# Holding more of a two-round decode kernel's last heads on the chip: values in PSUM, a shorter ring, a second kept record tail

## The chip, the cores and the metric

The kernel runs on one core of a Trainium2 chip. The metric is the device time of one execution in microseconds (us), the median of the runs shown. PE is the matrix engine (PEld its weight loads), DVE the vector engine, ACT the scalar engine, SP the engine that issues the loads.

## The reference

One token for each of 4 sequences goes through attention and an MLP, and then through the same two layers, with the same weights and caches, once more. Cut to what is computed:

```python
def _A_ref(x, k_cache, v_cache, wq, wo):       # 32 heads of 128, the last W = 1024 cached positions
    q = (x @ wq) by heads
    scores = einsum("bhqd,bhkd->bhqk", q, k[-W:]) * (Dh ** -0.5)
    return (einsum("bhqk,bhkd->bhqd", softmax(scores), v[-W:])) by rows @ wo
def _B_ref(x, w1, w2):
    return maximum(x @ w1, 0) @ w2             # 640 -> 1728 -> 640
for _ in range(2):
    x = x + _A_ref(_layernorm(x), k_cache, v_cache, wq, wo)
    x = x + _B_ref(_layernorm(x), w1, w2)
```

All numbers are f32. One head's query weights, keys, values and output weights for all four sequences make one record: 128 partitions of 9472 columns (`REC`), 4.85 MB. There are 32 records, so a round reads 155 MB of them and 8.85 MB of MLP weights.

## The kernel before

**Storage.** SBUF holds five whole records (`slot0` to `slot4`), a `ring` of 6912 columns and `kept`, the last 2176 columns of one more record. In a record the columns run `WQ` (640), `K` (4096), `V` (4096), `WO` (640). Head h of round 0 lies in slot h mod 5.

**Order.** Round 0 takes heads 0 to 31. Heads 27 to 31 stay in the five slots, so round 1 takes them first, and then 0 to 26. Round 0 therefore loads 32 records and round 1 loads 27, of which head 26 lacks the 2176 columns from `KEPT` on, which `kept` has held since round 0.

**Per head** the loop in the body (L421 to L434) does: scores of the next head (PE, `sc_ps`, 16 matmuls in the trace's count), its softmax (DVE maximum, ACT exponential), the values of this head (PE, `o_ps`), `picks` (four DVE operations that collect the blocks of `o_ps`), the query of the head after next (PE, `misc`), a transposing matmul, the output projection into `acc`, and the softmax weights of the next head (DVE). So the K part of a record is read one loop step before its V part. `busy` adds matmuls whose result nobody reads; in round 1 they stand in the first three steps only (L429).

**Loads.** `items` is the list of all loads in the order in which they are issued, all on SP's queue. `pump` issues the first one as soon as its place is no longer `live`; `done` takes columns off the list when the code that reads them last has been written. A load into used columns waits on the chip for that last reader. SP works in order: a load that waits holds up all loads behind it.

**Between the rounds** the MLP weights go through the ring (`MLP_RING`, eleven loads). Behind them come the first records of round 1: parts of head 0 go to the ring (`IN_RING`), and the rest of head 0 and heads 1 to 5 go, piece by piece, to the places that heads 27 to 31 leave (`places`); the last piece, the end of head 5, takes the ring. Head 6 is the first whole record again, in slot 2 (`home`), where head 27 was. Until then slot 2 holds pieces of heads 0, 1 and 2.

**PSUM** has eight banks of 512 columns: `sc_ps0` and `sc_ps1` (two each), `t_ps`, `o_ps`, `acc`, `misc`.

Of the kernel before, what the change touches and what calls it, by code (L numbers as in the profile page):

```python
# [58 lines left out]
RING = 4 * FF  # L59
KEPT = WO - 3 * 512  # L60

MLP_RING = [("w1", 1, 0), ("w1", 1, FF), ("w1", 1, 2 * FF), ("w1", 1, 3 * FF), ("w1", 1, 0), ("w2", 10, 1728),
            ("w2", 11, 3328), ("w2", 11, 5088), ("w2", 10, 0), ("w2", 8, 1728), ("w2", 4, 3008)]

IN_RING = [(512, 1664, 3648), (1664, 3712, 4800), (3712, 5248, 0), (0, 128, 1536), (5248, 6272, 1728),
           (6272, 6784, 2752), (128, 512, 3264)]
IN_SLOT = 6784
# [4 lines left out]
LATE = 5  # L72
# [24 lines left out]
def decode_kernel(ctx: ExitStack, tc: tile.TileContext, xf, rec, w1, w2, out):  # L97
# [24 lines left out]
    slot = [sb.tile([P, REC], F32, name=f"slot{i}") for i in range(NS)]  # L122
    ring = sb.tile([P, RING], F32, name="ring")
    kept = sb.tile([P, REC - KEPT], F32, name="kept")

# [41 lines left out]
    at = {("rec", 1, LAST - 1): [(KEPT, REC, "kept", 0)]}  # L167
    live = []
    buffers = dict(enumerate(slot)) | {"ring": ring, "kept": kept}

    def load(key, src, lo, hi, buf, col):
        items.append((key, src, lo, hi, buf, col))
# [4 lines left out]
    def ending(r, hs, late):  # L177
        a, b, c = hs[-3:]
        end = WO if late else REC
        last = WO if late else KEPT  # L180
        for h, lo, hi in ((a, 0, V), (b, 0, V), (a, V, end), (c, 0, V), (b, V, end), (c, V, V + VH), (c, V + VH, last)):
            piece(r, h, lo, hi)
        if late:
            for h in hs[-1:] + hs[-LATE:-1]:
                piece(r, h, WO, REC)
# [5 lines left out]
    for h in hs[1:-3]:  # L191
        piece(0, h, 0, KEPT if h == LAST - 1 else WO if h >= H - LATE else REC)
        if h == LAST - 1:
            piece(0, h, KEPT, REC, "kept", 0)
    ending(0, hs, True)
    loaded = {"w1": 0, "w2": 0}
    for name, size, col in MLP_RING:
        n, loaded[name] = loaded[name], loaded[name] + size * {"w1": FF, "w2": FD}[name]
        load((name, 0), {"w1": w1, "w2": w2}[name], n, loaded[name], "ring", col)
# [6 lines left out]

    for lo, hi, col in IN_RING:
        piece(1, new[0], lo, hi, "ring", col)
# [3 lines left out]
    stream = [(new[0], IN_SLOT, REC)] + [(h, 0, REC) for h in new[1:6]]  # L212
    for buf, lo, hi in places:
        while stream:
            h, c, end = stream[0]
            cut = max(x for x in [*CUTS, end] if x <= min(end, c + hi - lo))
            if cut <= c:
                break
            piece(1, h, c, cut, buf, lo)
            lo += cut - c  # L220
            stream[:1] = [(h, cut, end)] if cut < end else []
    for h in new[6:-3]:
        piece(1, h, 0, REC)
    ending(1, hs, False)
    for ks in W1_SLOT:
        load(("w1", 1), w1, ks[0] * FF, (ks[-1] + 1) * FF, home(LAST + 1, 0), ks[0] * FF)
    n = 0
    for size in W2_SLOT:
        load(("w2", 1), w2, n * FD, (n + size) * FD, home(LAST + 2, 0), n * FD)
# [23 lines left out]
    def done(key, lo, hi):  # L253
# [3 lines left out]
        for x, y, buf, col in pieces(key):  # L257
            a, b = col + max(lo, x) - x, col + min(hi, y) - x
            if a < b:
                rest = []  # L260
                for bb, u, v in live:
                    if bb != buf or v <= a or b <= u:
                        rest.append((bb, u, v))
                    else:
                        rest += [(bb, p, q) for p, q in ((u, a), (b, v)) if p < q]
                live[:] = rest
        pump()

# [4 lines left out]
    def busy(n, to=sc_ps[1], groups=1, h=LAST):  # L273
# [5 lines left out]
    def center(fill):  # L279
# [3 lines left out]
        if fill:  # L283
            busy(256, groups=fill)
        pe.matmul(misc[:, :B], sums.to_broadcast([P, P]), pick, start=True, stop=True)
        if fill > 1:
            busy(128, groups=2)
# [6 lines left out]
    def deviation(rows, bias, scale):  # L294

        pe.matmul(o_ps[:, 8:8 + B], ones.to_broadcast([P, P]), squares, start=True, stop=True)
        dve.tensor_tensor(mrt, o_ps[:, 8:8 + B], rows, op=OP.mult)
# [13 lines left out]
    def scores(r, h, s, first=False):  # L311
        key = ("rec", r, h)
        for i in range(2):
# [4 lines left out]
            if first and i == 0:  # L318
                deviation(of_batch, eps_dh, float(DH))
                act.activation(unused, eps, AF.Exp)  # L320
# [50 lines left out]
    def mlp(r):  # L371
# [3 lines left out]
        for k in range(KB):  # L375
            for j in range(NB):
                pe.matmul(h_ps[32 * j:32 * j + B, :FQ], xblock(k), cols(("w1", r), k * FF + FQ * j, FQ),
                          start=(k == 0), stop=(k == KB - 1))
            done(("w1", r), k * FF, k * FF + FF)
# [12 lines left out]
        key = ("w2", r)  # L392
        sizes = W2_SLOT if r else [size for name, size, _ in MLP_RING if name == "w2"]
        first = 0
        for i, size in enumerate(sizes):
            for s in range(first, first + size):
                m, n = TILES[s]
                w = cols(key, s * FD, FD)
# [5 lines left out]
            done(key, first * FD, (first + size) * FD)  # L404
# [5 lines left out]
    for r in range(2):  # L410
# [4 lines left out]
        if r:  # L415
            busy(256, groups=2)
        scores(r, hs[0], 0, True)
        softmax(0, True)
        query(r, hs[1])
        weights(0)  # L420
# [20 lines left out]
        values(r, hs[-1], 1, (1, 0))  # L441
        output_T(late - 2, by_act=True)
        picks(1)
# [50 lines left out]
```

## Time and profile before

| | us |
|---|---|
| median of 3 runs | 715.53 (715.3 to 715.67) |
| span of the profiled execution (first to last instruction) | 713.9 |
| busy: PE / DVE / ACT | 518.8 / 357.4 / 93.3 |
| share of the 16 DMA engines that SP's queue took | 99.0% |

The runs are timed from outside and lie 1.6 us above the profiled execution's span; a difference found in the span is carried over to the runs as it is. The profile page gives, by 40 slices, how busy each engine was and which share of its full clock PE was granted. The chain of waits follows the work that ended last back to the start. The timeline has single instructions with their start and duration, and windows give an engine's busy time, PE's granted clock and the DMA rate for any stretch. Line 89 (or 86) is the line of a helper through which every instruction is recorded, so instructions are told apart by their tiles.

### The profile page before, as it was taken

The numbers are of one execution on the slowest core, as the hardware profiler recorded it, in microseconds if no ns is written. First come the engines' busy times: TensorE is split into PE (matmuls) and PEld (weight loads), VectorE is DVE, ScalarE is ACT, GpSimd is POOL, SyncE is SP. The second block draws the span as 40 slices with busy tenths as digits, with TensorE's granted clock in tenths as the row PEclk, the third lists the DMA queues.
The fourth block names the chain that finished last, engine by engine and source line by source line (L and its number), as shares of the span: only waits on it lengthen the run. The fifth ranks groups of instructions, "written<-read, shape, count | busy, mean of one in ns | idle before, by whom it ended". The sixth has DMA issues, their size and how long they took to land.

```text
span 713.9 us, 8959 instructions
## 1 busy us (share of the span) xinstructions
PE 518.8 (73%) x3716; PEld 210.9 (30%) x3716; DVE 357.4 (50%) x1007; ACT 93.3 (13%) x147; POOL 1.1 (0%) x9
## 2 busy tenths in 40 slices
PE   4466858666785766868889998477767767686868
PEld 2131323223232231323224343132222313232323
DVE  3335445544454545446642887535444454445752
ACT  1201010110110101011111222101010110101111
POOL 0000000000000000000000000000000000000000
PEclk9768686877678677577899999857886687668989
DMA  9999999999999999999999999999999999999996
GB/s 374 442 437 430 425 436 440 429 419 442 438 432 423 434 438 437 417 442 422 424 406 408 428 429 429 442 438 423 430 439 436 427 430 434 437 430 423 429 424 274
DMA packets 16633, 303.38 MB, mean 425 GB/s; under 512 B 1856, under 2 KB 2384, under 8 KB 6736
## 3 DMA queue, kind: packets, MB, share of 16 engines
q1 hardware_dynamic: 16560, 302.80, 99.0%
q8 instruction: 29, 0.48, 0.2%
q14 instruction: 12, 0.10, 0.0%
q10 hardware_dynamic: 32, 0.01, 0.0%
HBM read 302.72 MB, written 0.08 MB: 424 GB/s over the span
## 4 chain that ended last, share of the span: by engine, by line
DMA 79%; PE 17%; DVE 2%; issue 1%; SPq 0%; ACT 0%
DMA slot<-rec 76%; PE sc_ps L89 6%; PE misc L89 5%; PE o_ps L89 4%; DMA ring<-w 3%; PE acc L89 3%; DVE scratch L89 1%; DVE oTs L89 1%; DVE small L89 0%; SPq L89 0%; DVE t_ps L89 0%; SPq L86 0%; DVE xT L89 0%; ACT oTs L89 0%; DVE qT L89 0%
## 5 line engine op out<-in xcount | busy, mean ns | idle before, releaser
L89 PE MATMUL misc<-xT,slot 128*128 128x4 f32 x630 | 103.2, 291 | 154.5 <-DMA slot<-rec 154.3
L89 PE MATMUL sc_ps<-slot,qT 128*4 128x512 f32 x1008 | 196.7, 920 | 1.0 <-DVE qT L89 1.0
L89 PEld LDWEIGHTS misc<-xT,slot 128*128 128x128 f32 x630 | 97.7, 240 | 210.8 <-DMA slot<-rec 199.1
L89 ACT ACTIVATE sc_ps<-sc_ps,small 128x1024 f32<-128x1024 f32 (+1 forms) x68 | 76.6, 1127 | 555.3 <-DVE small L89 554.8
L89 PE MATMUL o_ps<-slot,scratch 128*16 128x512 f32 x964 | 135.1, 672 | 3.0 <-DVE scratch L89 3.0
L89 DVE TENSOR_REDUCE small<-sc_ps 128x1 f32<-128x1024 f32 x64 | 78.3, 1223 | 73.9 <-PE sc_ps L89 73.9
L89 DVE STREAM_TRANSPOSE t_ps<-sc_ps 128x512 f32<-128x512 f32 x128 | 93.2, 728 | 2.1
L89 DVE COPY qT<-misc 128x4 f32<-128x4 f32 x64 | 10.2, 160 | 166.1 <-PE misc L89 166.1
L89 PEld LDWEIGHTS o_ps<-slot,scratch 128*16 128x16 f32 x964 | 32.7, 117 | 128.4 <-issue 79.0
L89 DVE SCALAR_TENSOR_TENSOR scratch<-o_ps,of_block,scratch 128x128 f32<-128x128 f32 x186 | 65.2, 351 | 6.6
L89 PEld LDWEIGHTS sc_ps<-slot,qT 128*4 128x4 f32 x1008 | 33.5, 115 | 84.1 <-issue 73.1
L89 PE MATMUL acc<-slot,oTs 128*4 128x160 f32 x488 | 36.5, 387 | 14.3 <-DVE oTs L89 14.0
L89 DVE TENSOR_SCALAR scratch<-o_ps,of_block 128x128 f32<-128x128 f32 x62 | 21.7, 351 | 34.1 <-PE o_ps L89 34.1
L89 PE MATMUL o_ps<-pick,scratch 128*128 128x4 f32 x124 | 29.1, 305 | 4.8 <-DVE scratch L89 4.8
L89 DVE TENSOR_TENSOR scratch<-t_ps,mrt 128x64 f32<-128x64 f32 x128 | 28.8, 225 | 4.7
L89 PEld LDWEIGHTS o_ps<-pick,scratch 128*128 128x128 f32 x124 | 26.1, 260 | 8.8 <-DVE scratch L89 7.5
L89 PE MATMUL sc_ps<-slot,small 128*1 128x256 f32 (+2 forms) x56 | 17.7, 462 | 0.0
L89 DVE COPY oTs<-o_ps 128x4 f32<-128x4 f32 x60 | 9.7, 162 | 14.8 <-PE o_ps L89 13.9
L89 DVE TENSOR_SCALAR mrt<-of_batch,small 128x4 f32<-128x4 f32 x64 | 14.7, 230 | 2.2
L89 DVE STREAM_TRANSPOSE scratch<-small 128x32 f32<-128x32 f32 x64 | 12.9, 201 | 2.4 <-ACT sc_ps L89 2.4
L89 PEld LDWEIGHTS acc<-slot,oTs 128*4 128x4 f32 x488 | 6.9, 84 | 19.5 <-DVE oTs L89 19.1
L89 ACT ACTIVATION_READ_ACCUMULATOR sc_ps<-sc_ps,small 128x1 f32 x64 | 12.2, 191 | 0.0
(71 smaller groups left out, 113.6 us busy)
## 6 DMA issues: line engine op xcount, KB each, us to landing
slot<-rec SPq DMA_DIRECT2D x43, 4736.0 KB, 30.7
slot<-rec SPq DMA_DIRECT2D x12, 2368.0 KB, 29.6
slot<-rec SPq DMA_DIRECT2D x2, 4416.0 KB
slot<-rec SPq DMA_DIRECT2D x2, 2304.0 KB, 18.4
ring<-w SPq DMA_DIRECT2D x5, 864.0 KB, 10.7
slot<-rec SPq DMA_DIRECT2D x2, 2112.0 KB, 19.0
slot<-rec SPq DMA_DIRECT2D x2, 2048.0 KB, 41.4
slot<-rec SPq DMA_DIRECT2D x4, 1024.0 KB, 20.3
```

The source lines that it names most:

```text
L89: r = build(*args, **kwargs)
```

## The change

1. `kept2`, a second tail of 2176 columns, takes the end of head 23 in round 0. Round 1 then loads head 23 without these columns.
2. The ring shrinks from 6912 to 4832 columns.
3. After the last values of round 0, `park` copies 1536 columns of head 31's values from slot 1 to PSUM (ACT, 1024 columns to `sc_ps1`, 512 to `o_ps`). Their place in slot 1 (`spare`) takes MLP weights and parts of head 0. At the start of round 1 `unpark` copies the columns to slot 2, into the K part that head 27 has just been read from (ACT 512 columns, DVE twice 512, and DVE clears `o_ps`). Head 31 reads them there.
4. The MLP's two weight arrays become one, `wm`, loaded in twelve pieces through ring and spare place; the lists of places follow. The end of `places` changes: columns of slot 2 that `unpark` used, and the spare columns of slot 1, are filled last, after head 31, with parts of head 5.
5. Six output projections of round 0 are kept for its end instead of five (`LATE`), head 26's among them.
6. What `busy`, `center` and `deviation` write goes to `misc` and `t_ps`, since `sc_ps1` and `o_ps` are taken.

```diff
-RING = 4 * FF
+RING = 4832
+PARKED = 1536
-LATE = 5
+LATE = 6
...
+    kept, kept2 = (sb.tile([P, REC - KEPT], F32, name=n) for n in ("kept", "kept2"))
...
-    at = {("rec", 1, LAST - 1): [(KEPT, REC, "kept", 0)]}
+    at = {("rec", 1, LAST - 1): [(KEPT, REC, "kept", 0)], ("rec", 1, LAST - 4): [(KEPT, REC, "kept2", 0)]}
+    spare = home(H - 1, 0)
...
     places = [(old[i], lo, hi) for i, lo, hi in (
-        (0, 0, K), (0, K, K + VH), (0, K + VH, V), (1, 0, K + VH), (1, K + VH, V), (0, V, WO), (0, WO, REC), (2, 0, V),
-        (1, V, REC), (3, 0, V), (2, V, REC), (4, 0, V), (3, V, REC), (4, V, REC))] + [("ring", 0, RING)]
+        (0, 0, K), (0, K + 1024, K + VH), (0, K + VH + 512, V), (1, 0, K + VH), (1, K + VH, V), (0, V, WO), (0, WO, REC),
+        (2, 0, V), (1, V, REC), (3, 0, V), (2, V, REC), (4, 0, V), (3, V, REC), (4, V + PARKED, REC),
+        (0, K, K + 1024), (0, K + VH, K + VH + 512), (4, V, V + PARKED))] + [("ring", 0, RING)]
...
     for h in new[6:-3]:
-        piece(1, h, 0, REC)
+        piece(1, h, 0, KEPT if h == LAST - 4 else REC)
...
+    def park(i):
+        if i == 0:
+            act.copy(sc_ps[1], slot[spare][:, V:V + 1024])
+        else:
+            act.copy(o_ps, slot[spare][:, V + 1024:V + PARKED])
+            free(spare, V, V + PARKED)
+            pump()
+
+    def unpark(i):
+        b = home(LAST, 0)
+        a = [K, K + 512, K + VH][i]
+        if i == 0:
+            act.copy(slot[b][:, a:a + 512], sc_ps[1][:, :512])
+        else:
+            dve.tensor_copy(slot[b][:, a:a + 512], [sc_ps[1][:, 512:], o_ps][i - 1])
+        live.append((b, a, a + 512))
+        if i == 2:
+            dve.memset(o_ps, 0.0)
```

SP's list at the point where whole records begin again in round 1. Before, the piece into the ring is the last of head 5, and head 6 follows into slot 2:

```order
L89 DMA slot1_71<-rec 128x4736
L89 DMA slot0_70<-rec 128x4224
L89 DMA slot0_70<-rec 128x512
L89 DMA ring_75<-rec 128x4224
L89 DMA slot2_72<-rec 128x9472
L89 DMA slot3_73<-rec 128x9472
```

And now; the two pieces of 1024 and 512 columns into slot 2 are keys of head 5 (the second half of its positions):

```order
L96 DMA slot1_71<-rec 128x3200
L96 DMA slot2_72<-rec 128x1024
L96 DMA slot2_72<-rec 128x512
L96 DMA slot1_71<-rec 128x1536
L96 DMA ring_77<-rec 128x3200
L96 DMA slot2_72<-rec 128x9472
L96 DMA slot3_73<-rec 128x9472
```

The load of head 6 is now behind two pieces of head 5 in the same slot, so it has to wait until PE has done the scores of head 5; before, the last reader of what slot 2 held was head 1's output projection.

DVE at the first softmax of round 1, before:

```order
L89 TENSOR_REDUCE small_69<-mrt_68 128x1
L89 TENSOR_REDUCE small_69<-sc_ps0_77 128x1
L89 RECIPROCAL small_69<-small_69 128x1
L89 TENSOR_TENSOR small_69<-small_69 128x1
L89 COPY qT_64<-misc_82 128x4
L89 STREAM_TRANSPOSE scratch_62<-small_69 128x32
```

And now:

```order
L96 TENSOR_REDUCE small_69<-mrt_68 128x1
L96 COPY slot2_72<-sc_ps1_79 128x512
L96 TENSOR_REDUCE small_69<-sc_ps0_78 128x1
L96 RECIPROCAL small_69<-small_69 128x1
L96 TENSOR_TENSOR small_69<-small_69 128x1
L96 COPY qT_64<-misc_83 128x4
L96 COPY slot2_72<-o_ps_81 128x512
L96 MEMSET o_ps_81 128x512
L96 STREAM_TRANSPOSE scratch_62<-small_69 128x32
```

One copy now stands ahead of the maximum over the scores, and a copy and a clearing stand between the copy of the next query and the first operation of the softmax weights.

More of the change, by code (lines that the diff above doesn't have):

```diff
@@ L191, in decode_kernel @@
     for h in hs[1:-3]:
-        piece(0, h, 0, KEPT if h == LAST - 1 else WO if h >= H - LATE else REC)
+        piece(0, h, 0, KEPT if h in (LAST - 4, LAST - 1) else WO if h >= H - LATE else REC)
+        if h == LAST - 4:
+            piece(0, h, KEPT, REC, "kept2", 0)
         if h == LAST - 1:
-            piece(0, h, KEPT, REC, "kept", 0)
+            piece(0, h, KEPT, WO, "kept", 0)
     ending(0, hs, True)
[L196 to L199, printed above, removed]
+    for lo, hi, buf, col in MLP_RING:
+        load(("w", 0), wm, lo, hi, buf, col)
     hs = order[1]
```

96 lines of the change are left out of this document (59 added, 37 removed).

## The prediction

> **What bounds the kernel now.** I read the page first, for the loads against everything else, then windows for their rate, then the chain and the timeline where round 1 starts.
>
> ```profile
> span 713.9 us, 8959 instructions
> ...
> DMA  9999999999999999999999999999999999999996
> ...
> q1 hardware_dynamic: 16560, 302.80, 99.0%
> ```
>
> The loads never stop: 302.80 MB, 99% of the 16 DMA engines over the whole span. Two windows give their rate, in the last column (GB/s; before it the DMA share and PE's granted clock):
>
> ```profile
> 40.00:300.00 260.00, 183.70 (x1204) 74.31 (x1196) 125.45 (x346) 29.78 (x46) 0.00 (x0) 0.74 1.00 432
> 0.00:453.20 453.20, 333.38 (x2394) 135.19 (x2398) 233.23 (x660) 62.04 (x97) 1.12 (x9) 0.80 1.00 427
> 370.00:380.00 10.00, 8.83 (x76) 2.17 (x74) 1.03 (x3) 2.32 (x5) 0.00 (x0) 1.00 0.98 398
> ```
>
> With whole records the rate is 432 GB/s, so one record of 4.85 MB takes 11.2 us. The time is bytes divided by rate, plus every moment in which the queue is empty. Such a moment hardly exists before; the nearest to one is in the MLP between the rounds (0.98).
>
> One stretch works the other way round: heads 27 to 31 need no loads, so at the start of round 1 PE and DVE set the pace and the loads run ahead into the places that they leave. The chain shows where that ends:
>
> ```profile
> 437.81 0.76 PE acc L89 x8
> 438.56 0.02 issue
> 438.58 27.80 DMA slot<-rec
> 466.38 0.04 issue
> 466.42 2.30 PE misc L89 x10
> ```
>
> At 438.58 head 1's projection frees slot 2, SP issues head 6, the first whole record, and its data land 27.80 us later. Of these 27.80 us only 11.2 are its own transfer; the rest is the queue ahead of it. That lead is what the change touches.
>
> **The bytes saved.** `kept2` spares round 1 2176 columns x 512 B = 1.114 MB. At 432 GB/s that is **2.58 us**. All other bytes stay, the weights in `wm` too. Nothing else in the change shortens the loads.
>
> **The new wait.** Head 6 now goes to slot 2 behind keys of head 5, and is issued only when the scores of head 5 are done. When is that, and when is the queue empty?
>
> PE's rows (start, duration; `sc_ps` are scores, `o_ps` values):
>
> ```profile
> 431.92 1.90 PE L89 MATMUL sc_ps<-slot,qT 128*4 128x512 f32 x16
> 438.30 3.30 PE L89 MATMUL sc_ps<-slot,qT 128*4 128x512 f32 x16
> 445.87 1.90 PE L89 MATMUL sc_ps<-slot,qT 128*4 128x512 f32 x16
> 452.04 1.90 PE L89 MATMUL sc_ps<-slot,qT 128*4 128x512 f32 x16
> ```
>
> These are the scores of heads 2, 3, 4 and 5. The last end at 453.94; heads follow each other every 6.17 us (445.87 to 452.04), and the waits of PE from 400 to 455 name no load, so this is a pace of PE and DVE that the loads don't set.
>
> Up to the last piece of head 5 the list before holds 188,608 KB = 193.1 MB. The window 0 to 453.20 at 427 GB/s is 193.5 MB: averaged over the engines, the queue reaches head 6 at 453.2, give or take 0.5 from the rounding. The changed list has the same bytes up to there (`kept2` saves behind it). So **the queue is empty at about 453.2, and the load that should follow is issued at about 454**: a lead of 14.6 us becomes less than nothing. Heads 7 and 8 are behind head 6 on SP and wait with it, though slots 3 and 4 are free by then; once it is issued, three records follow at once, and the queue is full again. So the loss is paid once.
>
> What does a restart cost from issue? Rows for an empty queue are the start and the end of the program (chain of the start, then the page of issues, us to landing last):
>
> ```profile
> 0.81 0.38 SPq L86
> ...
> 2.18 35.08 DMA slot<-rec
> ```
>
> ```profile
> out<-scratch SPq DMA_DIRECT2D x1, 80.0 KB, 1.6
> ```
>
> The small store lands after 1.6 us, 0.2 of them its transfer at 432 GB/s: 1.4. The first four loads (two of 2368 and two of 4736 KB, 14.55 MB, 33.7 us at that rate) are issued from 0.81 and land at 37.26: 2.8. The second holds the lag of the slowest engine, which a running queue has as well. I take 2.0 us, between them, and keep 1.4 and 2.8.
>
> [...]
>
> **What moves PE's 453.94.** Four small edits lie ahead of it:
>
> ```profile
> 364.13 0.16 ACT L89 COPY oTs<-o_ps 128x4 f32<-128x4 f32 x1 [4.86 <-PE o_ps L89]
> 369.66 1.28 ACT L89 ACT_TABLE_LOAD   x1 [5.37 <-DVE small L89]
> 390.95 0.29 ACT L89 ACTIVATE small<-small 128x1 f32<-128x1 f32 x1 [13.36 <-DVE small L89]
> 393.12 1.18 ACT L89 ACTIVATE sc_ps<-sc_ps,small 128x1024 f32<-128x1024 f32 x1 [0.35 <-DVE qT L89]
> 390.70 0.16 DVE L89 TENSOR_REDUCE small<-mrt 128x1 f32<-128x4 f32 x1
> 391.53 1.22 DVE L89 TENSOR_REDUCE small<-sc_ps 128x1 f32<-128x1024 f32 x1 [0.67 <-PE sc_ps L89]
> 394.44 0.21 DVE L89 STREAM_TRANSPOSE scratch<-small 128x32 f32<-128x32 f32 x1 [1.35 <-ACT sc_ps L89]
> 396.04 0.73 DVE L89 STREAM_TRANSPOSE t_ps<-sc_ps 128x512 f32<-128x512 f32 x1
> ```
>
> - `park`: no row is an ACT copy of this size; the exponential over 128x1024 takes 1.18, so 1.2 and 0.65 for the two. They fall into ACT's idle 4.86 and 5.37 us around 364: nothing. Without that cover the first would delay `oTs`, at most 1.2. The spare place is free near 365, when three weight loads are still queued.
> - `unpark`: a DVE copy of 128x512 lies between 0.16 (four columns) and 0.73 (the transpose of 512); I take 0.7. The first fills the gap from 390.86 to 391.53 and overhangs by about 0.1. The second, with the clearing of `o_ps` (no row; up to another 0.7), lies in the 1.35 us in which DVE waits for the exponential: 0 to 0.1. ACT's copy, 0.65 from about 390.1, ends before 390.95. Together **0.2** (0 to 0.7).
> - The ring and the spare place hold 6368 columns for weights where the ring held 6912, 0.64 us of transfer less. In the MLP SP then issues later against a queue that already had 0.98; the last weights can land up to 1 us later, though the late projections and fillers are waiting for loads there anyway. I take **0.1** (0 to 1.0). Idle time of the queue itself in that stretch costs nothing more, because it is empty at 453 in any case.
> - The sixth late projection, the merged weights and the other targets of the fillers change no sum: the same matmuls in the same idle time.
>
> Sum, against the profiled execution: 453.94 + 0.3, issue 0.06 after it, restart 2.0: data flow again at 456.3 where they flowed on at 453.2. That is 3.1 lost and 2.58 saved, **+0.5 us**, if PE meets the same clock.
>
> **PE's clock.** It need not. The row at 438.30 took 3.30 us where its like take 1.90, 1.4 us more. Windows of 3.41 us (clock in the column before the DMA share):
>
> ```profile
> 389.93:393.34 3.41, 2.91 (x28) 1.71 (x28) 1.85 (x6) 2.01 (x4) 0.00 (x0) 1.00 1.04 404
> 393.34:396.75 3.41, 3.41 (x20) 0.67 (x16) 2.17 (x6) 1.07 (x2) 0.00 (x0) 0.50 1.02 416
> 417.23:420.65 3.42, 2.74 (x32) 1.78 (x35) 2.80 (x11) 1.11 (x2) 0.00 (x0) 1.00 1.03 436
> 420.65:424.06 3.41, 3.41 (x33) 1.39 (x25) 3.05 (x8) 0.85 (x1) 0.00 (x0) 1.00 1.02 432
> 434.30:437.71 3.41, 2.83 (x24) 1.61 (x16) 2.67 (x9) 1.29 (x2) 0.00 (x0) 1.00 1.00 430
> 437.71:441.13 3.42, 3.32 (x24) 0.87 (x28) 2.36 (x8) 0.00 (x0) 0.00 (x0) 0.50 0.97 409
> 451.37:454.78 3.41, 3.15 (x38) 1.05 (x41) 3.06 (x9) 0.00 (x0) 0.00 (x0) 1.00 1.10 472
> ```
>
> The clock halves for whole windows on a grid of 3.41 us (393.34 + 13 x 3.413 = 437.71), here behind windows that hold much of the pause between a head's values and the next scores, 2.55 us in which PE has only small matmuls (449.49 to 452.04 in the rows). The busy column counts those too, so it doesn't show it. Where do windows lie against that pause?
>
> ```profile
> 415.15 1.90 PE L89 MATMUL o_ps<-slot,scratch 128*16 128x512 f32 x16
> 433.63 1.90 PE L89 MATMUL o_ps<-slot,scratch 128*16 128x512 f32 x16
> 447.59 1.90 PE L89 MATMUL o_ps<-slot,scratch 128*16 128x512 f32 x16
> ```
>
> The window that started 1.2 us before the values' end (434.30 against 435.53) was followed by a slow one; one that started 0.2 after it (417.23 against 417.05) was not, nor one 1.5 before it (447.95 against 449.49). So about 1.3 of 3.41 us of positions are bad. Two windows are 6.83, a head 6.17: the grid moves 0.66 per head, meets a bad position at the latest after five heads, is thrown back about two heads by the 1.4 us lost, and meets one again about three heads later. Six heads without fillers precede the scores of head 5. From a chance position that makes mostly two slow windows; the profiled execution had one, plus the one at 393.3, which I price at 0.35 because the values behind it waited for DVE's weights in any case. Before, none of this reached the end, since the queue had 14.6 us of lead. Now it does. I take two and none at 393: +0.5 + 1.4 - 0.35 = **+1.6 us**, so 715.5 + 1.6 = **717.1**.
>
> **The rivals.** 0.2% of this kernel is 1.43 us, about what a measurement of it can tell from no change.
>
> - *One slow window, as in the profile.* +0.2 without the one at 393, +0.5 with it: 715.7 to 716.0. For it: the one execution that is shown. Against: the count above. [...]
> - *Three slow windows, or one across the scores of head 5 themselves.* +1.6 + 1.4: about 718.5. Possible from positions that are bad at the first head.
> - *Faster: the queue hardly empties.* No slow window at all and a restart of 1.4: PE's scores end at 453.94 - 1.4 - 0.35 + 0.3 = 452.5, data flow at 454.0, 0.8 lost and 2.58 saved: -1.8, 713.7. It decides at about 1.1 us lost for a measurable gain. Against it: the drift argument leaves hardly a position without a slow window.
> - *The saving comes but the ring costs.* Weights land 1 us late and PE's pace with them, over the forecast: 718.1. Or the tail of head 23 isn't spared: +2.6 more; the list of loads speaks against that.
>
> **How the numbers follow.** Forecast (two slow windows) 0.45, one 0.20, three 0.22, hardly empty 0.10, ring 0.03. The forecast lies so near the bound that I give 0.27 of its 0.45 to slower and 0.18 to no change. Faster 0.10, same 0.18 + 0.20 = 0.38, slower 0.27 + 0.22 + 0.03 = 0.52. Range: from the one-window case with the short restart and no delay, 715.7 - 0.8 = 714.9, to three windows with 0.5 of the ring's cost, 719.0. The faster case and a tail above stay out. Its cases lie in steps of 1.4 us, so runs of the changed kernel should differ more among themselves than the 0.37 us before.
>
> **What would show it.** The SP row of the first whole record into slot 2 stands 0.06 behind PE's scores of head 5, near 454 to 456, no longer behind a projection at 438.6. The DMA share falls for 2 to 5 us there, and PE then waits for a load until about 468 to 470. The queue moves 301.7 MB. ACT's and DVE's copies take 0.6 to 1.2 us and the maximum at 391.53 starts 0.1 to 0.2 later. I am wrong if the share doesn't fall at 454 (the queue was longer than I think), if it falls in the MLP by several us, or if runs agree within 0.4 us while the wait is there.

## The result and the profile after

| | before | after |
|---|---|---|
| median, us | 715.60 (715.30 to 715.76, 5 runs) | 719.26 (718.38 to 720.90, 5 runs) |
| ratio | | 1.0053, 95% interval 1.0040 to 1.0065 |
| profiled execution: span | 713.9 | 716.6 (its time 718.40) |

The change makes the kernel 3.7 us slower by the medians and 2.7 us by the spans of the profiled executions. The forecast was 717.1, its range ended at 719.0. One execution of the kernel before, 769.65 us at a granted clock of 0.55, is in none of the numbers here.

The page after, in the rows that answer those of before:

```profile
span 716.6 us, 8970 instructions
...
DMA  9999999999999999999999999899999999999997
...
q1 hardware_dynamic: 16560, 301.69, 98.7%
```

The queue moves 1.11 MB less, as it should, and its row of tenths has one dip, in slice 26 of 40 (448 to 466 us). Microsecond windows there (last column GB/s):

```profile
453.00:454.00 1.00, 1.00 (x10) 0.95 (x9) 0.93 (x3) 1.00 (x2) 0.00 (x0) 1.00 1.03 441
454.00:455.00 1.00, 0.42 (x3) 0.30 (x2) 0.56 (x5) 0.02 (x1) 0.00 (x0) 1.00 0.84 358
455.00:456.00 1.00, 0.89 (x16) 0.43 (x20) 0.93 (x5) 0.00 (x0) 0.00 (x0) 1.00 0.51 218
456.00:457.00 1.00, 1.00 (x12) 0.22 (x8) 0.93 (x3) 0.00 (x0) 0.00 (x0) 1.00 0.27 106
457.00:458.00 1.00, 1.00 (x16) 0.27 (x12) 0.96 (x3) 0.00 (x0) 0.00 (x0) 1.00 0.00 0
458.00:459.00 1.00, 1.00 (x12) 0.08 (x4) 0.84 (x2) 0.00 (x1) 0.00 (x0) 1.00 2.04 568
```

From 454 on the share of the 16 engines that are busy falls step by step (0.84, 0.51, 0.27), and from 457 to 458 no packet starts. (A packet counts in the window in which it starts, so a share can exceed 1.) The chain of waits names the cause; before, a projection at 437.81 stood here, and 27.80 us of load behind it:

```profile
455.57 1.79 PE sc_ps L96 x16
457.37 14.08 DMA slot<-rec
471.49 2.30 PE misc L96 x10
```

Head 5's scores end, SP issues head 6, and PE gets the record 14.08 us later; 11.2 of them are its own transfer. This is the predicted wait. But the issue stands at 457.37, where 455.3 was forecast. PE's rows show why:

```profile
391.07 1.03 PE L96 MATMUL sc_ps<-slot,qT 128*4 128x512 f32 x8
...
433.56 3.60 PE L96 MATMUL sc_ps<-slot,qT 128*4 128x512 f32 x16
...
447.80 3.31 PE L96 MATMUL sc_ps<-slot,qT 128*4 128x512 f32 x16
...
455.38 1.90 PE L96 MATMUL sc_ps<-slot,qT 128*4 128x512 f32 x16
```

Two scores at half clock, as forecast (3.60 and 3.31 us instead of 1.90; the granted clock is 0.50 from 433.56 to 436.97 and 0.51 from 447.20 to 450.60). But round 1's first scores start at 391.07; before, they did 2.0 us earlier:

```profile
389.12 1.03 PE L89 MATMUL sc_ps<-slot,qT 128*4 128x512 f32 x8
```

So the two late microseconds come from ahead of round 1, from the MLP. Windows of that stretch, before and then after:

```profile
362.00:400.00 38.00, 34.79 (x332) 12.81 (x326) 13.66 (x47) 7.19 (x13) 0.00 (x0) 0.96 1.01 410
376.00:388.00 12.00, 11.38 (x146) 4.45 (x138) 1.99 (x7) 1.08 (x3) 0.00 (x0) 1.00 1.02 410
```

```profile
362.00:400.00 38.00, 31.72 (x320) 11.76 (x315) 13.11 (x41) 7.13 (x14) 0.00 (x0) 1.00 1.00 385
376.00:388.00 12.00, 9.91 (x132) 4.05 (x133) 0.87 (x2) 1.08 (x3) 0.00 (x0) 1.00 0.99 369
```

25 GB/s less over 38 us are 0.95 MB, 2.2 us of transfer. The DMA share (the column ahead of the rate) hides it: 1.01 against 1.00. A share near 1 is no proof that the queue is full; the rate tells more. The chain of that stretch, before and after:

```profile
380.02 5.84 DMA ring<-w
385.86 0.04 issue
385.90 0.53 PE acc L89 x8
```

```profile
377.46 6.71 DMA ring<-wm
384.21 1.39 PE acc L96 x34
```

Before, the last load of the MLP stands there, and 0.5 us of PE behind it. Now it is the largest, 2560 columns (1280 KB, 3.0 us of transfer), issued at 377.46. PE waits for the whole of it, then does 34 matmuls, the rest of the group, three more groups and the unread matmuls between them. The next load into these columns is issued at 385.78, when PE has nearly finished the group; before, the columns came free in smaller parts.

**Lead.** For each load I counted how much of the queue lay ahead of it when it was issued: the bytes listed ahead of it, less the bytes that the trace's packets had moved by then (a packet under way counts by the part of its time that has passed), divided by 432 GB/s. Of the 18 loads issued between 365 and 392 us before, none had less than 2.0 us of lead; the least was 2.1. After the change 3 of 14 had 1.1 to 1.7. The rate dips right behind these loads. After the change, behind the issues at 377.46 (lead 1.1) and at 385.78 (1.3):

```profile
376.50:378.00 1.50, 1.46 (x8) 0.26 (x8) 0.08 (x1) 0.50 (x2) 0.00 (x0) 1.00 0.98 408
378.00:380.00 2.00, 1.61 (x26) 0.74 (x27) 0.78 (x2) 0.57 (x2) 0.00 (x0) 1.00 0.97 318
386.50:388.00 1.50, 1.50 (x28) 0.75 (x28) 0.00 (x0) 0.00 (x0) 0.00 (x0) 1.00 1.06 332
```

Before, at the same place, and behind the load with the least lead (368.87, 2.1):

```profile
378.00:380.00 2.00, 1.80 (x30) 0.66 (x24) 0.07 (x1) 0.00 (x0) 0.00 (x0) 1.00 0.99 401
369.50:371.00 1.50, 1.50 (x10) 0.17 (x2) 0.08 (x1) 1.33 (x2) 0.00 (x0) 1.00 0.88 323
```

By 390 the changed kernel's queue had lost 1.7 us more than the one before, and 1.1 of them in the three stretches behind its short-lead loads (368 to 371, 378 to 380, 386 to 388). Smaller dips (372 to 373, 382 to 384) stand behind loads with more lead, so the count isn't the whole account, and the bound of 2.0 us is chosen with the traces at hand. The experiments ask whether short lead is what costs.

### The profile page after: what moved, and what is told of

Read it like the earlier page. It is cut to its first block, busy times and chain, and to the rows that moved or that the text cites. A ratio compares the mean times of both kernels' runs of the same rounds, so it can differ in the third digit from the quotient of the medians.

```text
span 716.6 us, 8970 instructions
## 1 busy us (share of the span) xinstructions
PE 514.7 (72%) x3718; PEld 210.3 (29%) x3718; DVE 358.6 (50%) x1010; ACT 95.5 (13%) x150; POOL 1.1 (0%) x9
## 3 DMA queue, kind: packets, MB, share of 16 engines
q1 hardware_dynamic: 16560, 301.69, 98.7%
## 4 chain that ended last, share of the span: by engine, by line
DMA 78%; PE 18%; DVE 3%; issue 1%; another core or an unknown queue 1%; ACT 0%; SPq 0%
DMA slot<-rec 72%; PE sc_ps L96 5%; PE misc L96 5%; PE o_ps L96 5%; DMA ring<-wm 3%; DMA slot<-wm 3%; PE acc L96 3%; DVE scratch L96 2%; DVE oTs L96 1%; DVE small L96 0%; ACT sc_ps L96 0%; PE t_ps L96 0%; DVE t_ps L96 0%; DVE mrt L96 0%
## 5 line engine op out<-in xcount | busy, mean ns | idle before, releaser
L96 PE MATMUL misc<-xT,slot 128*128 128x4 f32 x640 | 104.7, 290 | 157.0 <-DMA slot<-rec 156.7
L96 PE MATMUL o_ps<-slot,scratch 128*16 128x512 f32 x958 | 133.2, 661 | 3.7 <-DVE scratch L96 3.2
L96 PE MATMUL acc<-slot,oTs 128*4 128x160 f32 x470 | 34.7, 381 | 13.5 <-DVE oTs L96 13.2
L96 PE MATMUL misc<-slot,small 128*1 128x512 f32 (+1 forms) x40 | 19.2, 570 | 0.0
```

Of the source, the lines that this page charges most:

```text
L96: r = build(*args, **kwargs)
```

## The experiments

The first four take the change apart. Each was timed in turns with the kernel before, whose median was 715.49 to 715.63 in these sessions.

**1. The homes of round 1 rotated by one slot.** Head 6 then goes to slot 3, which holds nothing of head 5.

```diff
-        return h % NS if not r or h >= LAST else (h - 6 + LAST) % NS
+        return h % NS if not r or h >= LAST else (h - 5 + LAST) % NS
...
-        load(("w", 1), wm, ks[0] * FF, (ks[-1] + 1) * FF, home(LAST + 1, 0), ks[0] * FF)
+        load(("w", 1), wm, ks[0] * FF, (ks[-1] + 1) * FF, home(LAST + 2, 0), ks[0] * FF)
...
-        load(("w", 1), wm, W2 + n * FD, W2 + (n + size) * FD, home(LAST + 2, 0), n * FD)
+        load(("w", 1), wm, W2 + n * FD, W2 + (n + size) * FD, home(LAST + 3, 0), n * FD)
```

> The changed kernel with one line of placing turned: in round 1 heads 6, 7, 8, 9, 10 go to slots 3, 4, 0, 1, 2 instead of 2, 3, 4, 0, 1, so that the first whole record goes to a slot that head 5's keys don't occupy. All copies, the short ring and the kept tails stay. Theory W (the wait of head 6's load for head 5's scores empties the queue, 3.5 to 6 us): the queue stays busy around 455, the runs agree within 0.5 us, and the time is 715.6 - 2.58 saved + 2.6 that the queue already lost before 452 (it reached the last piece of head 5 at 452.05, where the kernel before reached the same byte at 449.4), so 715.2 to 716.0. Rival P (PE's later pace after the MLP or the copies set the end, the wait only stands beside it): the time stays at 718.4 to 721.

Measured: 716.74 (715.06 to 719.75, 12 runs), ratio 1.0020 (1.0006 to 1.0033). Head 6 is issued at 448.04 with 7.6 us of queue ahead of it, and the rate doesn't dip there (444 GB/s from 453 to 463, against 294 after the change). So the wait is real and was worth 2.5 us. But with it gone and 2.58 us saved the kernel is still not faster than before, and its runs spread over 4.7 us where 0.5 was expected. There is a second loss.

**2. The wait alone, in the kernel before.** 512 columns of slot 2's keys and 2560 of slot 1's values are held back for the end of head 5, as in the change; ring, lists and bytes stay.

```diff
-        (0, 0, K), (0, K, K + VH), (0, K + VH, V), ...
+        (0, 0, K), (0, K + 512, K + VH), (0, K + VH, V), ...
...
-        ... (3, V, REC), (4, V, REC))] + [("ring", 0, RING)]
+        ... (3, V, REC), (4, V + 2560, REC), (0, K, K + 512), (4, V, V + 2560))] + [("ring", 0, RING)]
```

> The kernel before with nothing but the order of two places changed: 512 columns of slot 2 are filled late, with keys of head 5, so that head 6's load waits for head 5's scores; 2560 columns of slot 1 are held back to make the pieces come out. Bytes, ring and copies are as before. Theory W: scores end at 453.9 (with the profiled clock), data flow again 2.0 later at 456.0 against 453.2, so 2.8 lost: 718.4, and 717.0 to 720.0 in steps of 1.4 by PE's slow windows, runs apart by more than 1 us. Rival P: 715.6, runs within 0.5.

Measured: 720.85 (718.12 to 721.29, 6 runs), ratio 1.0062 (1.0049 to 1.0076). In its chain:

```profile
453.57 1.73 PE sc_ps L89 x16
455.30 14.01 DMA slot<-rec
```

First scores of round 1 at 389.03, as before, so this is the wait by itself: 5.3 us by the medians, more than W's 720.0 allowed, and 3.5 in the profiled execution.

**3. Ring and lists alone.** The change without `kept2`, parking and late pieces in slots 1 and 2; the spare place is 1536 columns of the ring's own.

```diff
-RING = 4832
+RING = 4832 + 1536
...
-            buf, col = spare, V + col
+            buf, col = "ring", 4832 + col
...
-                if r:
-                    unpark(0)
...
-            park(0)
```

> The changed kernel without the second kept tail, without parking and with no late piece in slot 2: the spare place of 1536 columns is part of the ring (4832 + 1536 = 6368 columns), so the lists of weights and of head 0 are the changed ones, in the room that they have there. Head 23 is loaded whole in both rounds. Theory R (the 544 columns less and the changed lists make the queue idle between 362 and 400): 715.6 + 2.6 = 718.2, runs within 0.5, weights' end about 2 us later than before. Rival K (the copies that free the spare place come late, and the room itself is enough): 715.6, weights' end as before.

Measured: 720.04 (716.75 to 721.84, 7 runs), ratio 1.0055 (1.0035 to 1.0075). The edit that was priced at 0.1 us costs 4.4 by the medians, 1.6 in the profiled execution, which was among the shortest of the seven. R said 718.2 with runs within 0.5; the runs spread over 5.1 us. Head 6 has 13.5 us of lead here, so nothing of it is the wait. The window of the MLP reads as in the changed kernel:

```profile
362.00:400.00 38.00, 31.29 (x320) 11.64 (x315) 10.98 (x38) 5.90 (x11) 0.00 (x0) 1.00 0.99 385
```

**4. Unread matmuls between the heads,** to take the half-clock windows away.

```diff
+            if r and NS - 2 <= n < NS + 5:
+                pe.matmul(sc_ps[n % 2][:1, :512], ones, kept[:, :512], start=True, stop=True)
             output_T(max(i, 0))
```

> The changed kernel with one filler matmul of 512 columns, which reads the kept tail, in each of the eight loop steps of round 1 that have none (steps 3 to 9 lie before head 5's scores). Theory H (the spread and a part of the loss are PE's half-clock windows behind pauses): no half-clock window between 400 and 455, head 5's scores start at about 452.2 instead of 455.4, head 6's data flow at 456.1 where the queue would reach them at 455.8: 715.7 to 716.5, runs within 0.6. Rival: the half-clock windows stay or don't matter: 718.4 to 721, spread of 2 us.

Measured: 718.45 (717.96 to 720.43, 5 runs), ratio 1.0042 (1.0030 to 1.0054). From 400 to 460 us, after the change and then with the unread matmuls (clock in the column ahead of the DMA share):

```profile
400.00:460.00 60.00, 54.16 (x484) 23.21 (x480) 48.49 (x140) 12.65 (x19) 0.00 (x0) 0.94 0.97 404
```

```profile
400.00:460.00 60.00, 56.34 (x496) 23.20 (x492) 48.60 (x140) 12.96 (x20) 0.00 (x0) 1.00 0.98 409
```

```profile
448.40 1.90 PE L96 MATMUL sc_ps<-slot,qT 128*4 128x512 f32 x16
...
455.02 1.90 PE L96 MATMUL sc_ps<-slot,qT 128*4 128x512 f32 x16
```

They keep the clock whole, but a head now takes 6.62 us instead of 6.17. Six heads give back 2.7 of the 3.1 us that the two slow scores cost (3.60 and 3.31 us instead of 1.90); head 6 is issued at 457.01 instead of 457.37. A miss, 2 us above what H said: the cure costs nearly what the illness does.

**5. The largest loads cut in two.** If a big load is the trouble, the changed kernel gets better with two halves, each released by its own group of matmuls.

```diff
-W2_RING = [5, 8, 9, 16, 5, 8, 3]
+W2_RING = [5, 8, 9, 8, 8, 5, 8, 3]
...
-            ... (W2 + 3520, W2 + 6080, "ring", 0), ...
+            ... (W2 + 3520, W2 + 4800, "ring", 0), (W2 + 4800, W2 + 6080, "ring", 1280), ...
...
-            ... (1664, 4224, "ring", 0), ...
+            ... (1664, 2688, "ring", 0), (2688, 4224, "ring", 1024), ...
```

> The changed kernel with its largest weight load (2560 columns, 16 tiles) cut into two of 1280, each released by its own group of matmuls, and the 2560-column load of the first new head behind it cut into 1024 and 1536. Ring, kept2, park and the wait on head 5 stay. Theory G (the grain of the loads makes round 1 start late: a load must land whole before its first matmul and be used up whole before the next one may be issued): the first scores of round 1 start at 389.8 or before instead of 391.07, the queue loses 1.5 us or more less between 362 and 400, and the time is 717.2 to 718.2. Rival C (the capacity does it, 6368 columns where 6912 were): first scores within 0.4 of 391.07 and 718.5 to 720.

Measured: 718.34 (717.37 to 720.18, 5 runs), ratio 1.0042 (1.0030 to 1.0054); first scores at 390.87. The median is 0.9 below the change's, but the two intervals overlap (1.0040 to 1.0065 there), and the first scores are hardly earlier, as C said. 1 of 17 loads has under 2 us of lead (1.3). Not decided by this run.

**6. The same cut in the rotated kernel.**

> The rotated homes together with the cut loads; kept2 whole (2176 columns, 2.58 us saved), ring and spare place 6368 columns. Theory G: the queue loses at most 0.8 us more than before between 362 and 400, so 713.0 to 714.2 and less spread than the rotated kernel with whole loads (715.06 to 719.75). Rival C: 716.7, runs from 715 to 720, as that kernel.

Measured: 714.72 (713.86 to 716.38, 11 runs), ratio 0.9990 (0.9982 to 0.9999): 2.0 better than uncut, with about half its spread, though above G's 714.2. The first version that beats the kernel before, by 0.8 us only; 1 of 17 loads has under 2 us of lead (1.7), and 393 GB/s stand in its window.

**7. One big load in the kernel before.** The other way round, at the whole ring:

```diff
-            ... ("w2", 10, 0), ("w2", 8, 1728), ("w2", 4, 3008)]
+            ... ("w2", 18, 0), ("w2", 4, 3008)]
```

> The kernel before, with the ring of 6912 columns and one edit: its weight loads of 10 and 8 tiles are joined into one of 18 tiles (2880 columns), so 4 loads follow later in one step. Theory G (grain): first scores of round 1 0.8 to 2 us later than 389.1, time 716.2 to 718, and runs differ by more than 1 us among themselves. Rival C (capacity): 715.6, within 0.4.

Measured: 717.18 (715.95 to 722.23, 11 runs), ratio 1.0034 (1.0018 to 1.0049). As G said, the size of one load, at 6912 columns, costs 1.6 us; and it makes runs differ by 6. (One unread matmul falls away with the join; experiment 9, which puts four in, has the same median.) PE's rows at the joined load:

```profile
386.08 2.75 PE L89 MATMUL acc<-ring,scratch 128*4 128x160 f32 x42 [2.49 <-DMA ring<-w]
...
391.98 1.03 PE L89 MATMUL sc_ps<-slot,qT 128*4 128x512 f32 x8
```

PE waits 2.49 us, then works through the load, here at half clock:

```profile
383.10:386.50 3.40, 0.91 (x16) 0.33 (x18) 0.00 (x0) 0.00 (x0) 0.00 (x0) 1.00 0.97 387
386.50:389.90 3.40, 3.33 (x46) 1.73 (x34) 0.58 (x2) 0.00 (x0) 0.00 (x0) 0.50 1.02 398
```

**8. Room.** Rotated, with 512 columns given back from `kept2` to the ring: 6880 columns, loads of at most 1728.

```diff
-RING = 4832
+RING = 5344
+KEPT2 = WO - 2 * 512
...
-W2_RING = [5, 8, 9, 16, 5, 8, 3]
+W2_RING = [7, 10, 9, 10, 10, 8]
```

> The changed kernel with round 1's homes rotated by one slot (head 6 no longer waits for the scores of head 5), 512 columns given back from kept2 to the ring (1664 columns kept, ring and spare place 6880 columns together), and loads of at most 1728 columns in the MLP. Saved 0.852 MB, 1.97 us at 432 GB/s. C and G both say that the MLP then runs as before: first scores of round 1 within 0.5 of 389.1 and 713.4 to 714.4, runs within 1 us. If the runs still spread over 3 us or more, what varies is neither grain nor capacity but what the two rotated kernels share: parking, six late projections, merged weights.

Measured: 716.06 (714.77 to 719.32, 12 runs), ratio 1.0009 (1.0000 to 1.0018); first scores at 390.94, 383 GB/s. Both theories missed. Nearly the whole ring of before and no load above 1728 columns, and the loss is there. So neither the room nor the largest load is the quantity by itself. In this list the weights of the MLP's first half and of its second share a load, and 2 of 14 loads have under 2 us of lead (1.8). What the kernels with a loss share is short lead.

**9. to 11. Is it PE's clock?** Unread matmuls fill PE's wait for the big load: four in the kernel before with the joined load, three each in the rotated kernel and in the one with ring and lists alone. A fourth kernel is the rotated one with the unread matmuls of experiment 4 between its heads.

```diff
         for i, size in enumerate(sizes):
+            if r == 0 and i == 3:
+                for _ in range(4):
+                    busy(512)
```

> The kernel before with its two weight loads joined (2880 columns), and four matmuls of 512 columns that nobody reads put ahead of the matmuls that wait for that load; PE waited 2.49 us there, four of them take 1.7. Theory M (the runs spread because the wait starves PE's clock: the window of 3.41 us behind it goes to half clock, the matmuls that release the ring take twice their time, and the queue dries further): no half-clock window between 380 and 392, first scores at 391.0 or before (391.98 without fillers), 715.8 to 717.0 with all runs within 1.5 us. Rival D (the queue's 16 engines run dry by chance when little is queued, whatever the clock): 717.2, runs from 716 to 722 as without fillers.

> The rotated kernel with whole loads, and three unread matmuls of 512 columns ahead of the matmuls that wait for the 2560-column weight load. Theory M: 715.0 to 716.2 with all runs within 1.5 us (715.06 to 719.75 without). Rival D: 716.7, runs over more than 4 us.

> The kernel with the changed ring and lists alone (no kept2, no parking, homes as before; 716.75 to 721.84, median 720.04), with three unread matmuls of 512 columns ahead of the matmuls that wait for the 2560-column weight load. Here no later load is short of lead (head 6 has 13.5 us queued ahead of it, head 9 17), so the stretch between the rounds is all that can vary. Theory M (PE's clock there makes the spread): all runs within 1.6 us, median 717 to 718.2. Rival D (the queue's engines run dry by chance): spread over 3.5 us, median 719.5 or more.

> The rotated kernel with one unread matmul of 512 columns in each of the steps 3 to 10 of round 1, which kept the clock full from 399 to 463 in the kernel with fillers and no rotation, and costs 0.43 us a head. Theory H (the rotated kernel's spread of 715.06 to 719.75 comes from half-clock windows between the heads of round 1): runs within 1.2 us. Theories M and D: the spread stays over 3 us, since head 6 is issued with 7.8 us queued ahead of it in the rotated kernel and late heads cost it nothing; median 716 to 717.

| kernel | median, range without | median, range with |
|---|---|---|
| before, joined load | 717.18, 715.95 to 722.23 | 717.07, 716.87 to 718.20 (8 runs) |
| rotated | 716.74, 715.06 to 719.75 | 716.26, 715.23 to 718.75 (11 runs) |
| ring and lists alone | 720.04, 716.75 to 721.84 | 719.32, 718.55 to 720.47 (5 runs) |
| rotated, between the heads | 716.74, 715.06 to 719.75 | 716.41, 714.75 to 719.28 (11 runs) |

M is half right. Where PE waited longest its clock made most of the spread, as far as 8 to 11 runs tell: 6.3 us fall to 1.3, and the window behind the wait keeps the whole clock (386.50 to 389.90: 1.00, where it was 0.50). With ring and lists alone 5.1 us fall to 1.9, over 7 and 5 runs. But no median falls by more than 0.7, so the clock is not the loss, and in the rotated kernel most of the spread stays. H fell: the windows between the heads don't matter once head 6 has lead.

**12. Six late projections alone,** the part of the ring edit that the above leave in.

```diff
-LATE = 5
+LATE = 6
...
-                piece(r, h, WO, REC)
+                if h == LAST - 1:
+                    piece(r, h, WO, REC, "kept", WO - KEPT)
+                else:
+                    piece(r, h, WO, REC)
...
-            piece(0, h, KEPT, REC, "kept", 0)
+            piece(0, h, KEPT, WO, "kept", 0)
```

> The kernel before with one edit: six late projections instead of five (the output weights of head 26 land in kept among the late pieces). Ring, lists and homes of before. If the ring and its lists are the cause (G and C): 715.6, all runs within 0.6. Rival L (the longer tail of late work before the weights, on PE and in the queue, makes round 1 start late): 716.6 or more, first scores at 389.8 or later instead of 389.1, and runs that differ by over 1.5 us.

Measured: 715.52 (715.28 to 716.90, 11 runs, ten of them up to 715.90), ratio 1.0001 (0.9992 to 1.0010), first scores at 389.03. Not the cause.

**13. and 14. Fine loads.** In the rotated kernel every weight load between the rounds is cut to at most 864 columns and every load of head 0 to 1024, each released by its own matmuls; the same in the kernel before, with its loads halved. (That makes 35 loads where the kernel of experiment 6 has 19, and 31 where before has 18; the expectations count too few.)

```diff
-W2_RING = [5, 8, 9, 16, 5, 8, 3]
+W2_RING = [5, 4, 4, 4, 5, 4, 4, 4, 4, 5, 4, 4, 3]
-MLP_RING = [(0, 1728, "ring", 0), (1728, 3456, "ring", 1728), (3456, 4752, "ring", 3456), (4752, 6048, "spare", 0),
+MLP_RING = [(0, 864, "ring", 0), (864, 1728, "ring", 864), (1728, 2592, "ring", 1728), (2592, 3456, "ring", 2592),
...
-            done(("w", r), k * FF, k * FF + FF)
+                if j % 2:
+                    done(("w", r), k * FF + FQ * (j - 1), k * FF + FQ * (j + 1))
```

> The rotated kernel with all loads between the rounds cut to at most 864 columns for the weights and 1024 for the first new head (29 loads where the rotated kernel with two cut loads has 20), each released by its own matmuls; the same unread matmuls as the changed kernel. Where the queue runs full a load ends some 0.05 us later than its bytes by 432 GB/s, so nine more loads cost about 0.5 us. Theory G: slack (queue ahead at issue) at least 2.8 us for nearly all loads between 365 and 392, losses of under 0.6 us beside those 0.5, 714.0 to 714.8, all runs within 2 us. Rival C (capacity sets the loss, whatever the grain): 715.0 to 716.5.

> The kernel before with its loads between the rounds cut in halves (29 where there were 18; ring of 6912 columns, the same order, each load released by its own matmuls). Its slack was 2.6 to 3.9 us there already and its losses small. Theory G: 715.4 to 716.2, eleven more loads at 0.05 us against a little less loss, all runs within 0.8 us. A rise of over 1 us would say that small loads cost more than the grain gives.

Measured: rotated and fine **713.89** (713.66 to 714.55, 11 runs), ratio 0.9977 (0.9968 to 0.9986); before with fine loads 716.25 (716.14 to 716.54, 11 runs), ratio 1.0011 (1.0001 to 1.0020). The first is the fastest kernel here, 1.7 us below the kernel before and 5.4 below the change, with the change's own smaller ring. Its window and its first scores:

```profile
362.00:400.00 38.00, 34.50 (x332) 12.77 (x329) 13.67 (x43) 8.00 (x14) 0.00 (x0) 1.00 1.03 401
```

```profile
389.72 1.03 PE L100 MATMUL sc_ps<-slot,qT 128*4 128x512 f32 x8
```

Each further load costs about 0.05 us (before with halves: 13 more, 0.7 us). That is the price where no lead is short; where it is, the grain is worth more: 16 more loads than in experiment 6 gain 0.8 us net. Beside each other, lead, rate and first scores from the profiled executions and the spread from all runs (the middle half, since the numbers of runs differ):

| kernel | loads with lead under 2.0 us, 365 to 392 | least lead | GB/s, 362 to 400 | first scores | middle half of the runs spans (runs) |
|---|---|---|---|---|---|
| before | 0 of 18 | 2.1 | 410 | 389.12 | 0.2 (128) |
| six late projections | 0 of 18 | 2.7 | 410 | 389.03 | 0.2 (11) |
| before, fine | 0 of 27 | 2.6 | 408 | 389.49 | 0.2 (11) |
| rotated, fine | 0 of 30 | 2.1 | 401 | 389.72 | 0.2 (11) |
| rotated, big loads cut | 1 of 17 | 1.7 | 393 | 390.44 | 0.7 (11) |
| room | 2 of 14 | 1.8 | 383 | 390.94 | 0.7 (12) |
| before, joined load | 2 of 14 | 1.5 | 383 | 391.98 | 2.0 (11) |
| after | 3 of 14 | 1.1 | 385 | 391.07 | 1.7 (5) |
| ring and lists alone | 3 of 14 | 0.9 | 385 | 391.37 | 3.5 (7) |
| rotated | 3 of 14 | 1.1 | 384 | 391.28 | 1.7 (12) |

The kernel before has single runs at 717.20 and 718.07 too, two of 128. The five traces with added unread matmuls (experiments 4 and 9 to 11), which are not in the table, have three such loads each and 374 to 388 GB/s.

**15. Fine loads, homes as changed.** What is the wait worth when the ring is mended?

> The changed kernel with the fine loads of the fastest kernel, but homes as changed, so that head 6 still waits for head 5's scores. If the wait has a cost of its own: 715.55 + 0.7 for the finer loads - 2.58 saved + 3.5 to 5.3 for the wait (one profile and the median of the wait alone) = 717.2 to 719.0, first scores at 389.8 as with fine loads and rotated homes, runs 1.4 us or more apart. If the wait is hidden once round 1 starts earlier: 713.9, within 1 us, as the rotated kernel with fine loads.

Measured: 717.57 (715.47 to 719.45, 12 runs), ratio 1.0026 (1.0015 to 1.0038), first scores at 389.62. Against the rotated kernel with fine loads the wait costs 3.7 us and brings the spread (4.0 us against 0.9). In the profiled execution (718.77, among the longest) two scores run at half clock, a third slow window falls on values (2.81 us at 422.30, where 1.90 is usual), and head 5's scores end at 457.45:

```profile
427.75 3.50 PE L100 MATMUL sc_ps<-slot,qT 128*4 128x512 f32 x16
...
441.88 3.25 PE L100 MATMUL sc_ps<-slot,qT 128*4 128x512 f32 x16
...
455.55 1.90 PE L100 MATMUL sc_ps<-slot,qT 128*4 128x512 f32 x16
```

## Why the prediction was wrong

**The failed step is the ring.** "In the MLP SP then issues later against a queue that already had 0.98; the last weights can land up to 1 us later ... I take 0.1." In the profile round 1 starts 2.0 us later (391.07 against 389.12), twice the upper bound. With 2.0 in place of 0.1 the forecast is 719.0, against 719.26 measured. By the medians the term is what the wait leaves of 3.66 measured plus 2.58 saved: 2.6 us with the wait at 3.68 (717.57 less 713.89), 3.7 with the wait at 2.52 (experiment 1). The prediction had this case among its rivals ("the saving comes but the ring costs"), but with a chance of 0.03 and 1 us as its price. I had counted columns: 544 fewer, 0.64 us of transfer. And I had read the share: the row with 0.98 has 398 GB/s beside it, where the queue moves 432 with whole records (40 to 300 us). What goes with the loss in these runs is the lead of each load, which fell from 2.1 us and more to 1.1 in the worst case, since the new lists have larger and fewer loads in less room. The rate dips right behind such loads, and finer loads in the same ring take most of the loss away (716.74 to 713.89 with rotated homes).

**One sentence of it was right and misled me.** "Idle time of the queue itself in that stretch costs nothing more, because it is empty at 453 in any case." So it was: the queue arrived 2.6 us later at head 6 and waited there the less. But the same late loads also move PE, and PE's time sets the issue of head 6. I costed the queue and forgot the reader of its data. In the profiled executions the parts nearly add up (3.5 for the wait alone and 1.6 for the ring alone, less 2.58, is 2.5; measured 2.7). By the medians they don't (5.3 and 4.4, less 2.58, would be 7.1; measured 3.7), and no trace shows one of the slower runs that lift those medians.

**The wait was right** in place and about right in size. It stands where it was said, SP 0.09 us behind head 5's scores (0.06 forecast), with heads 7 and 8 behind it. The data flow again about 1.9 us after the issue, traced back at 432 GB/s from the bytes that the packets moved later (forecast 2.0, bounds 1.4 and 2.8); with the wait alone it is 1.9 too. Windows from 440 to 462, after and then in the rotated kernel with fine loads, give the loss:

```profile
440.00:462.00 22.00, 16.95 (x147) 6.50 (x146) 16.27 (x47) 3.94 (x7) 0.00 (x0) 0.92 0.91 371
```

```profile
440.00:462.00 22.00, 16.30 (x144) 6.04 (x132) 15.35 (x42) 3.88 (x6) 0.00 (x0) 0.92 1.03 435
```

64 GB/s over 22 us are 1.41 MB, 3.3 us; the forecast, with its clock term, was 4.1. By the medians the wait is 2.5, 3.7 or 5.3 us (experiments 1, 15 and 2), so the forecast lies within what was measured, and no closer than that.

In its packets the restart reads so: the first packet starts 0.97 us after the issue at 457.37, and the first packets of the engines take 1.7 to 2.9 us where later ones take 1.4.

**The bytes were right:** 301.69 MB, 1.11 less.

**Parking and unparking cost less than forecast,** next to nothing where 0.2 was taken:

```profile
361.05 1.02 ACT L96 COPY sc_ps<-slot 128x1024 f32<-128x1024 f32 x1 [2.51 <-issue]
363.39 0.16 ACT L96 COPY oTs<-o_ps 128x4 f32<-128x4 f32 x1 [1.33 <-PE o_ps L96]
363.59 0.59 ACT L96 COPY o_ps<-slot 128x512 f32<-128x512 f32 x1
```

```profile
392.75 0.69 DVE L96 COPY slot<-sc_ps 128x512 f32<-128x512 f32 x1
393.48 1.23 DVE L96 TENSOR_REDUCE small<-sc_ps 128x1 f32<-128x1024 f32 x1
...
394.95 0.68 DVE L96 COPY slot<-o_ps 128x512 f32<-128x512 f32 x1
395.82 0.48 DVE L96 MEMSET o_ps<- 128x512 f32 x1 [0.18 <-DVE slot L96]
396.38 0.21 DVE L96 STREAM_TRANSPOSE scratch<-small 128x32 f32<-128x32 f32 x1
```

The forecast sizes were near (1.2 and 0.65 for ACT, 0.7 for DVE). The first ACT copy ends ahead of `oTs`, which still waits for PE. The maximum starts 2.41 us behind the first scores, as it did before (391.53 less 389.12), and the first operation of the softmax weights 5.31, against 5.32 before (394.44 less 389.12).

**The clock was right in number:** two slow windows, none at 393 (granted clock 1.00 from 389.20 to 396.02). That is the usual case and not the only one: of the 16 traces without unread matmuls between the heads, nine have two slow windows that begin between 400 and 455 us, two have one and five have three. That the grid's position is chance was my assumption; in the two traces it does differ: the first slow window behind 430 begins at 437.71 before and at 433.56 after, 1.2 windows of 3.41 us apart. That the changed kernel's runs spread was forecast too, but put down to these windows alone. Kernels without the wait spread as much when their lead is short.

**The sum, in the profile.** By the bytes that the queue had moved it reaches head 6 2.6 us late, loses 3.4 there and is spared 2.6: +3.4, against +2.7 in the spans. The rest comes back within the last 1 MB of loads, and I have no row that says how.

**What stays open:** why short lead makes runs differ, and with it the part of the medians that the traces don't show (4.4 us for ring and lists alone, 1.6 in its trace). PE's clock explains it for the joined load; in the rotated kernel it doesn't, and its head 8, issued with only 4.8 us of lead, was not tested apart. Nor was a long lead at a small ring with large loads, which the storage doesn't allow.

## What to carry to other kernels

Price a smaller staging buffer by the lead that each load has when it is issued, not by the columns that are lost: here the rate fell where loads were issued with about 2 us of queue or less ahead of them, close to the 1.9 us that an empty queue took to start again, and finer loads mended most of a smaller ring's loss for 0.05 us per extra load. When data come late, cost the engine that reads them as well as the queue, and follow it to the next load that it releases. Before columns are handed to the last reader in line, look which record is loaded over them next: rotating the homes by one slot was worth 2.5 to 3.7 us.

## What the runs showed of the hardware

- The DMA share stays at 0.99 to 1.00 in stretches that lose 6% of the rate (410 against 385 GB/s), and at 0.97 and 1.06 in the two dips to 318 and 332. The share alone doesn't show such a loss.
- One window of half clock came without an idle PE ahead of it. Of these two windows of the changed kernel the second is at half clock, and in the first, which comes ahead of it, PE is busy for 2.83 of 3.40 us:

```profile
443.80:447.20 3.40, 2.83 (x24) 1.61 (x16) 2.67 (x9) 1.30 (x2) 0.00 (x0) 1.00 0.98 412
447.20:450.60 3.40, 3.29 (x24) 0.89 (x28) 2.38 (x8) 0.00 (x0) 0.00 (x0) 0.51 1.00 413
```

  PE's gaps in the first are 0.6 us in all; no run here shows why the clock of the second is 0.51. One unread matmul of 512 columns per head (0.43 us) kept the clock whole from 400 to 460 (1.00, against 0.94 without).
